# Attention followed by a mixture of experts: gating in small steps inside the next batch's attention, global scores one slot ahead, another order in the software DMA queue, six y buffers

## The chip, the cores and the metric

The kernel runs on one core of a Trainium2 chip. The metric is the time of one execution on the device in microseconds (us), the median of several runs. Two numbers appear for a run: its time, and the span of its profile from the first to the last instruction, which is about 2 us shorter. Engines are called PE (TensorE matmul), DVE (VectorE), ACT (ScalarE), POOL (GpSimd) and SP (SyncE).

For one core, a run is called slow when it is over 1.5% above the fastest of the same kernel. Ratios use fast runs only. They are computed as the mean time of one kernel's fast runs over the mean of the other's fast runs in the same rounds, with a 95% interval, so a ratio is not quite the ratio of the medians quoted beside it. The experiments ran on three chips, called A, B and C here, and the kernel before was timed again on each.

## The reference, cut to what matters

```python
def _attn_ref(q, k, v, n_global, n_local):       # q, k, v: (4, 8, 768, 64) fp32
    ...
    keep = is_global | is_local                  # 8 global keys, 96 local ones (causal)
    ...                                          # bias by distance and head, softmax
    return np.matmul(a, v)

def _moe_ref(x, w_skip, w_gate, w1, w2):         # x: 3072 rows of 512
    do_compute = x @ w_skip > 0                  # the other rows are copied
    out = x.copy()
    e_idx = np.argmax(xc @ w_gate, axis=1)       # one of 8 experts
    ...                                          # gate_w: its softmax probability
    for e in range(E):                           # w1 (8,512,1024), w2 (8,1024,512)
        h = np.maximum(xc[mask] @ w1[e], 0.0)
        y[mask] = gate_w[mask, None] * (h @ w2[e])
    out[do_compute] = xc + y
```

Rows of one batch can be gated as soon as its attention is finished. The experts need the rows of all batches, because the rows of one expert come from everywhere.

## The kernel before

There are 16 attention units, one for each batch and pair of heads (`n` counts units, `hp` the pair within the batch `b`). Each unit has transposes of q and k, three score steps and two value steps. A value step writes rows to `xb`. When a batch is complete, SP writes its rows to DRAM (`x_out`), and during the next batch's units its rows are gated: `logits` (transposes and copies, three pieces), then `gate` and `place` as one block each. `place` turns the ranks of the rows into expert slots (`slot_ps`). `skip_out` scatters 128 finished rows to the output.

```python
    for n in range(NU):                          # NU = 16
        b, hp = units[n]
        if hp == 0:
            global_scores(b)                     # both halves, as the batch begins
        m, j = n + 4, n + 2
        ...                                      # scores(j, 0)
        values(n, 0)
        ...                                      # scores(j, 1), transposes(m, 1)
        if b > 0 and hp < 3:
            logits(b - 1, hp)
        ...                                      # scores(j, 2)
        values(n, 1)
        ...                                      # transposes(m, 0), loads
        if hp == HP - 1:
            x_out(b)
        if b > 0 and hp == 2:
            gate(b - 1)
        for _ in range(2):
            if skips:
                skip_out(skips.pop(0), "first")
        if b > 0 and hp == 3:
            gate_rest(b - 1)
            place((b - 1) * T, T, colid_i, gat_pool, ps_ms, "ms")
            skips += range((b - 1) * T, b * T)
```

For each expert, 256 slots are gathered from DRAM (`gather`, two indirect DMAs), transposed on PE (`xp`, copied to `xt`), multiplied by w1 (`hps`, then `ht`) and by w2 (`yps`). DVE adds the gated result to the row in `y`, and an indirect DMA scatters `y` to the output. Weights are loaded in halves of 1 MB after conversion to bf16. Eight halves are loaded during attention and eight late. Every gather, scatter and weight load is issued by GpSimd, in program order.

```python
    def expert(e, xt, rows, gate_, group):
        ...                                      # 4 times: hps (8 matmuls), Relu to ht
        for c in range(2):
            yps = ps_y.tile([128, DM], FP32, tag="yps", name="yps")     # 3 buffers
            ...                                  # 8 matmuls
            y = ffn.tile([128, DM], FP32, tag="y", name="y", bufs=4)
            ...                                  # DVE: y = yps * gate + xg
            put(nc.gpsimd.indirect_dma_start(    # scatter y to the output
                ...), group)

    def experts(group, first):
        rows, src, gate_ = slot_rows()
        for e in range(E):
            gather(e, src)
            if first and e % 2 == 1:
                for i in range(2):
                    load_half(2 * (E - 4) + e - 1 + i, wearly if e == 1 else wlate)
        xt = expert_in(0)
        for e in range(E):
            nxt = expert_in(e + 1) if e + 1 < E else None
            expert(e, xt, rows, gate_, group)
            if first:
                if e > 0 and e < 4:
                    for t in range(NT - T + 2 * e - 2, NT - T + 2 * e):
                        skip_out(t, group)
            xt = nxt
```

The softmax here doesn't subtract the row's maximum and nothing guards it: scores larger than these inputs give would overflow.

## Time and profile before

| | before |
|---|---|
| median of the first three runs | 234.59 us (234.57 to 235.47) |
| span of the profiled run | 234.0 us |
| last `xb` written (attention ends) | starts at 113.23 us |
| last gating ends (`slot_ps` of batch 3) | 126.95 us |
| first gather issued | 129.33 us |
| first matmul of expert 0 | 137.20 us |
| last `y` | starts at 221.03 us |

The page's rows below divide the span in 40 slices of 5.85 us. A digit is the busy share of a slice in tenths; PEclk is the granted TensorE clock.

```profile
span 234.0 us, 4720 instructions
...
PEclk9999997699758985598575559999965569999975
DMA  5999999999999999999960299999999633311110
GB/s 82 145 173 187 181 139 157 236 161 146 158 196 243 211 236 230 246 237 241 274 168 20 67 155 211 241 215 229 222 201 222 183 105 123 104 64 45 40 43 0
```

The DMA row is full from the second slice to about 117 us, nearly empty from 123 to 135 us (20 and 67 GB/s, the last gating and the first gathers), and full again until about 181 us. The windows show the hole in two stretches; the columns are the start and end, the length, the busy time of the engines, the granted clock, the DMA share and GB/s.

```profile
core 0: us, PE busy (x) PEld busy (x) DVE busy (x) ACT busy (x) POOL busy (x), PEclk, DMA share, GB/s
...
122.00:127.00 5.00, 0.38 (x9) 0.30 (x10) 4.41 (x19) 0.24 (x1) 0.21 (x1) 0.63 0.14 34
127.00:132.00 5.00, 0.53 (x6) 0.34 (x6) 1.25 (x10) 0.00 (x0) 2.06 (x3) 0.50 0.09 26
```

The view of waits gives who waited for whom: total us, number of waits, longest.

```profile
ACT g_sb L279 <- PE gp L276: 19.8, 8, 6.1
PE yps L613 <- DVE y L618: 19.5, 1, 19.5
POOL out_dram L482 <- DMA w<-in_moe_w_dram: 17.9, 5, 4.2
...
PE slot_ps L472 <- DVE oha L466: 14.4, 4, 3.9
...
PE rk_ps L411 <- DVE ohb L406: 8.5, 4, 2.7
```

`gp` are the global scores, `oha` and `ohb` are the serial chain of gating. In the attention stage PE stands for them because each gating block is a run of small DVE instructions with a matmul at its end. The 19.5 us wait is one single stop of PE. The chain of waits that ended last shows where it comes from (start, duration, what ran):

```profile
151.26 17.66 DMA w<-in_moe_w_dram
168.96 0.54 issue
169.73 17.81 DMA out_dram<-y,rows
187.66 0.76 DVE y L618
188.47 3.40 PE yps L613 x8
```

The `y` of expert 0 was computed at 144.17 and 145.90 us. Its scatter was issued only at 169.73 us, because GpSimd first had to issue all gathers and all late weights, and it waited for room in the queue (about 4 us at a time). It landed at 187.5 us. The fifth `y` had to wait for that landing, and PE waited for the fifth `y`.

One more view matters later: the PE timeline where the experts begin (start, duration, instruction, idle time before it and its releaser).

```profile
132.17 0.61 PE L593 MATMUL xp<-ident,xg 128*128 128x128 bf16 x4 [4.64 <-DMA xg<-x_rows,src]
134.22 1.12 PE L593 MATMUL xp<-ident,xg 128*128 128x128 bf16 x8 [1.43 <-DMA xg<-x_rows,src]
136.80 0.61 PE L593 MATMUL xp<-ident,xg 128*128 128x128 bf16 x4 [1.47 <-DMA xg<-x_rows,src]
137.20 5.20 PE L606 MATMUL hps<-xt,w 128*128 128x256 bf16 x32
```

PE is in program order, and the program has the transposes of expert 1 ahead of the first matmul of expert 0. The rows of an expert come in two halves. The first line is the first half of expert 0's rows, the second line is its second half together with the first half of expert 1's, and the third is the second half of expert 1's. So expert 0 starts 5.0 us after the first half of its own rows has come and 3.0 us after the second half, when expert 1's are there too.

### The profile page before, as it was taken

What the parts mean: (1) busy time and instruction counts of PE and PEld (TensorE: products, weight loads), DVE (VectorE), ACT (ScalarE), POOL (GpSimd) and SP (SyncE); (2) the same over time, 40 slices, a digit from 0 to 9 for tenths busy, and PEclk for the clock granted to TensorE, in tenths of its full rate; (3) what the DMA queues carried; (4) which work ended last, traced back from release to release, by engine and by line L of the source; (5) the groups of instructions that cost most, each with busy time, mean ns of one, the idle gap of its engine ahead of it and who ended that gap; (6) DMA issues with size and microseconds to landing.
All of it is one profiled execution on the core that took longest, in us unless ns stands there. A gap on an engine that the chain in (4) does not pass through costs nothing.

```text
span 234.0 us, 4720 instructions
## 1 busy us (share of the span) xinstructions
PE 150.0 (64%) x1877; PEld 106.2 (45%) x1877; DVE 108.5 (46%) x341; ACT 91.3 (39%) x144; POOL 112.1 (48%) x139
## 2 busy tenths in 40 slices
PE   1569995985769757695451179699800079999700
PEld 1445771764527645365451155566600046776400
DVE  7554996498845888478838021130000061232300
ACT  5865982893518935293030013223400004433200
POOL 8765596666572232641360775633436057333210
PEclk9999997699758985598575559999965569999975
DMA  5999999999999999999960299999999633311110
GB/s 82 145 173 187 181 139 157 236 161 146 158 196 243 211 236 230 246 237 241 274 168 20 67 155 211 241 215 229 222 201 222 183 105 123 104 64 45 40 43 0
DMA packets 50521, 38.25 MB, mean 163 GB/s; under 512 B 30276, under 2 KB 39492, under 8 KB 50496
## 3 DMA queue, kind: packets, MB, share of 16 engines
q0 software_dynamic: 45568, 34.62, 94.4%
q1 hardware_dynamic: 4928, 3.30, 5.5%
q8 instruction: 16, 0.26, 0.5%
q14 instruction: 9, 0.07, 0.1%
HBM read 54.68 MB, written 13.63 MB: 292 GB/s over the span
## 4 chain that ended last, share of the span: by engine, by line
DMA 30%; PE 25%; DVE 20%; ACT 9%; issue 6%; POOL 5%; POOLq 0%; ACTq 0%; DVEq 0%
DMA out_dram<-y,rows 8%; DMA w<-in_moe_w_dram 8%; PE yps L613 7%; DMA kr<-in_k_dram 6%; PE hps L606 6%; DMA xg<-x_rows,src 5%; DVE xb L346 4%; DVE a L315 4%; DMA qr<-in_q_dram 4%; PE gp L276 3%; ACT xts L376 3%; ACT a L301 3%; ACT a L309 3%; POOL xg L585 2%; DVE qt L255 2%
## 5 line engine op out<-in xcount | busy, mean ns | idle before, releaser
L609 ACT ACTIVATE ht<-hps 128x512 bf16<-128x512 f32 x32 | 19.1, 597 | 76.8 <-PE hps L606 76.8
L613 PE MATMUL yps<-w,ht 128*128 128x512 bf16 x128 | 30.6, 393 | 19.5 <-DVE y L618 19.5
L618 DVE SCALAR_TENSOR_TENSOR y<-yps,gate,xg 128x512 f32<-128x512 f32 x16 | 11.9, 750 | 65.8 <-PE yps L613 34.4
L482 POOL DMA_INDIRECT out_dram<-xb,skip_k x24 | 25.0, 1042 | 35.1 <-DMA w<-in_moe_w_dram 17.9
L315 DVE TENSOR_TENSOR a<-a,mask 128x896 bf16<-128x896 bf16 (+1 forms) x48 | 28.3, 590 | 18.7 <-ACT a L301 11.2
L301 ACT ACTIVATE a<-sc 128x896 bf16<-128x896 f32 x32 | 28.9, 924 | 8.7 <-PE sc L296 7.7
L621 POOL DMA_INDIRECT out_dram<-y,rows x16 | 15.7, 981 | 33.2 <-DVE y L618 23.4
L606 PE MATMUL hps<-xt,w 128*128 128x256 bf16 x256 | 30.8, 281 | 0.0
L613 PEld LDWEIGHTS <-ht 128*128 128x128 bf16 x128 | 12.9, 100 | 34.0 <-issue 21.5
L606 PEld LDWEIGHTS <-w 128*128 128x128 bf16 x256 | 25.6, 101 | 3.7
L585 POOL DMA_INDIRECT xg<-x_rows,src x16 | 15.6, 976 | 22.0 <-DMA w<-in_moe_w_dram 11.6
L97 POOL DMA_DIRECT2D vb<-in_v_dram x24 | 21.4, 903 | 6.7 <-DVE vb L93 2.5
L296 PE MATMUL sc<-qt,kt 64*128 64x224 bf16 x192 | 19.6, 293 | 3.1 <-ACT a L301 1.3
L333 PE MATMUL av<-vb,a 128*128 128x65 bf16 x192 | 19.3, 208 | 0.0
L340 PE MATMUL av<-vb,a 128*96 128x65 bf16 x160 | 18.5, 220 | 0.0
L346 DVE TENSOR_TENSOR xb<-av,rc 128x384 bf16<-128x384 f32 x32 | 17.8, 558 | 1.1
L333 PEld LDWEIGHTS <-a 128*128 128x128 bf16 x192 | 17.2, 118 | 0.0
L340 PEld LDWEIGHTS <-a 128*96 128x96 bf16 x160 | 15.8, 139 | 0.0
L376 ACT ACTIVATE xts<-xt_ps 128x1024 bf16<-128x1024 bf16 x11 | 11.3, 1030 | 10.0 <-PE xt_ps L369 9.7
L251 PE MATMUL tr<-ident,kr 96*64 96x96 bf16 x256 | 10.9, 243 | 6.5 <-DMA kr<-in_k_dram 6.5
L88 POOL DMA_DIRECT2D qr<-in_q_dram x16 | 10.4, 649 | 8.3 <-PE sc L296 3.5
L259 ACT ACTIVATE kt<-tr 128x768 bf16<-128x768 bf16 x16 | 13.0, 814 | 1.7 <-PE tr L251 1.7
(117 smaller groups left out, 221.0 us busy)
## 6 DMA issues: line engine op xcount, KB each, us to landing
w<-in_moe_w_dram POOLq DMA_DIRECT2D x16, 1024.0 KB, 18.9
kr<-in_k_dram POOLq DMA_DIRECT2D x16, 192.0 KB, 7.9
qr<-in_q_dram POOLq DMA_DIRECT2D x16, 192.0 KB, 7.8
vb<-in_v_dram POOLq DMA_DIRECT2D x24, 128.0 KB, 8.7
x_rows<-xb SPq DMA_DIRECT2D x4, 768.0 KB, 8.9
out_dram<-xb,skip_k POOLq DMA_INDIRECT x24, 10.0
xg<-x_rows,src POOLq DMA_INDIRECT x16, 12.3
out_dram<-y,rows POOLq DMA_INDIRECT x16, 2.7
```

Of the source, the lines that this page charges most:

```text
L97: nc.gpsimd.dma_start(out=vbs[b][:, t, :, 0:D], in_=v_r[b, t])
L296: nc.tensor.matmul(out=sc[:, hh, kk, 0:R * wp].rearrange("a (r p) -> a r p", r=R), lhsT=kt[rows, t * 128:(t + 1) * 128], rhs=qt[rows, :, t ...
L301: nc.scalar.activation(out=a[:, :, :].rearrange("a h (k p r) -> a h k p r", k=2, r=R), in_=sc[:, :, :, 0:W].rearrange("a h k (r p) -> a h ...
L315: nc.vector.tensor_tensor(out=a[:, :, 0:wid], in0=a[:, :, 0:wid], in1=m[:, :, 0:wid], op=ALU.mult)
L333: nc.tensor.matmul(out=av[:, jj, hh, :], lhsT=a_sbs[n, t // 2][:, hh, (t % 2) * W:(t % 2) * W + 128], rhs=vb[:, t, h, :], start=False, sto ...
L340: nc.tensor.matmul(out=av[0:NL, jj, hh, :], lhsT=a_sbs[n, p // 2][:, hh, c:c + NL], rhs=vb[:, p, h, :], start=False, stop=(jj == 2 and hh ...
L346: nc.vector.tensor_tensor(out=xb[:, 3 * u:3 * u + 3, 2 * hp * D:(2 * hp + 2) * D].rearrange("p j (h d) -> p j h d", h=2), in0=av[:, :, :, ...
L482: put(nc.gpsimd.indirect_dma_start(out=out[:, :], out_offset=bass.IndirectOffsetOnAxis(ap=skip_k[:, t:t + 1], axis=0), in_=xbs[t // T][:, ...
L585: nc.gpsimd.indirect_dma_start(out=xg[e][:, c, :], out_offset=None, in_=x_dram[:, :], in_offset=bass.IndirectOffsetOnAxis(ap=src[:, 2 * e ...
L606: nc.tensor.matmul(out=hps[:, j, :], lhsT=w1_sb[e][:, dc, c2 * 256 + j:(c2 + 1) * 256:2], rhs=xt[:, dc, :], start=(dc == 0), stop=(dc == D ...
L609: nc.scalar.activation(out=ht[:, c2, :, :], in_=hps[:, :, :], func=ACT.Relu)
L613: nc.tensor.matmul(out=yps[:, :], lhsT=ht[:, f // 2, f % 2, c * 128:(c + 1) * 128], rhs=w2_sb[e][:, f // 2, (f % 2) * DM:(f % 2 + 1) * DM] ...
```

## The change

The intent has four parts. Gating becomes a generator of small steps, and each attention unit takes three of them, between its own steps, so that the serial chain fills holes instead of making them. The global scores of the next batch are computed in the last unit of the batch before, which needs transposes five units ahead (`LEAD`) instead of four. In the expert part, only six experts' gathers and the weights of experts 4 to 6 are issued at once; those of experts 6 and 7 and the last weights come after the `y` of expert 0. And `y` has six buffers.

```diff
-    def global_scores(b):
+    def global_scores(b, u):                     # one half per call
...
+    def gating(b):                               # logits, gate, place, gate_rest
+        for s in range(3):
...
+            yield
...                                              # further steps, each ends with a `yield`
-    for n in range(4):
+    LEAD = 5
+    for n in range(LEAD):
...
     for n in range(NU):
         b, hp = units[n]
-        if hp == 0:
-            global_scores(b)
-        m, j = n + 4, n + 2
+        m, j = n + LEAD, n + 2
...
+        if hp == 3 and b + 1 < B:
+            global_scores(b + 1, 0)
+        next(side, None)
         values(n, 0)
...
-        if b > 0 and hp < 3:
-            logits(b - 1, hp)
+        if hp == 3 and b + 1 < B:
+            global_scores(b + 1, 1)
+        next(side, None)
...
         values(n, 1)
+        next(side, None)
...
-        if b > 0 and hp == 2:
-            gate(b - 1)
...
-        if b > 0 and hp == 3:
-            gate_rest(b - 1)
-            place((b - 1) * T, T, colid_i, gat_pool, ps_ms, "ms")
+        if hp == HP - 1:
+            x_out(b)
+            for _ in side:                       # what is left of the batch before
+                pass
+            side = gating(b)
...
-            y = ffn.tile([128, DM], FP32, tag="y", name="y", bufs=4)
+            y = ffn.tile([128, DM], FP32, tag="y", name="y", bufs=6)
...
-        for e in range(E):
-            gather(e, src)
-            ...                                  # two late halves after each odd e
+        fetch(0, 8)                              # gathers of experts 0 and 1, halves 8, 9
+        fetch(2, 10)
+        fetch(4, 12)
         xt = expert_in(0)
         for e in range(E):
             nxt = expert_in(e + 1) if e + 1 < E else None
             expert(e, xt, rows, gate_, group)
-            if first:
-                if e > 0 and e < 4:              # 2 skip scatters each
+            if e == 0:
+                fetch(6, 14)
+            if first and e >= 3:                 # 2 skip scatters each
```

## The prediction

> What bounds it now. Three stretches, from the timeline, the waits and the 40 slices (span 234.0 us).
>
> (a) Attention, to 116.9 us. A unit of batch 0 takes about 3.55 us with VectorE full. Batches 1 and 2, which also carry gating, take 29 us each (gp matmuls at 38.9, 67.0, 96 us), although VectorE is busy for only about 20.5 (windows). The holes: PE waits for ohb (8.5 us over four gatings) and for oha (14.4), ACT waits for gp (19.8 over eight). Behind this stands a second limit: the DMA row reads 9 tenths from 6 us to 117, and GpSimd waits for room in the one software queue (17.9 us "out_dram <- DMA w").
>
> (b) Last gating, 116.9 to 127.5 us, then the first gather at 129.3 and the first expert at 137.2: DMA nearly idle (20 and 67 GB/s).
>
> (c) Experts: 7.4 us each on a warm PE, but PE stands 19.5 us (from 168.9): the fifth y needs one of four buffers; expert 0's rows were computed at 144.2 but their scatter was issued at 169.7, behind all gathers and late weights, and landed at 187.5. Last scatter issued at 222.1, 12 us before the end.
>
> The change only moves work. Gating steps fill VectorE and PE holes: I estimate batches 1 and 2 at 22 to 23 us each, from the 20.5 us of VectorE; the last xb at about 98 to 101 instead of 113.8. One more unit in the prologue delays the first values by 2 to 3 us. The last gating is unchanged (10.6 us), so slots are ready near 110 instead of 127.5. But the queue still has the same bytes to move before the gathers; in before it is drained only at about 121. By the Trainium skill ("DMA: Bandwidth & Descriptors", Anatomy of one DMA) DMA engines do not wait on semaphores but consume their queues; the trace agrees (weights issued at 151.3 landed 17.7 us later). So I expect the gathers issued near 111 but landed near 122 to 125, and expert 0 near 125 instead of 137: 12 us gained, 8 more hidden behind DMA.
>
> Experts, as an estimate from the trace (half a weight 4.8 us of queue, a gather 0.75, a y scatter 1.2): queue order now is six gathered experts and w of 4 to 6, then y of expert 0, then expert 7. Its y lands near 162, y of expert 1 near 177. With six y and three yps buffers PE runs without a stop into expert 5, stands there 5 to 9 us instead of 19.5, and ends near 194 to 196 instead of 221. So 12 to 14 us gained here.
>
> Prediction: 209 us (11% faster), range 200 to 219. Faster by over 2% 0.97, within 2% 0.02, slower 0.01.
>
> Right if: the waits show yps<-y under 10 us and the wait for the y scatter after expert 2, not 1; PE's oha and ohb waits fall from 23 us to under 8 outside the last gating; the DMA row has no hole near 120 to 130; the first xp transposes come at 120 to 127. Wrong if: the two ms PSUM buffers, with rk held over two steps, stall the transposes so that batches stay at 27 us or more; q and k, needed a unit sooner, arrive late (DMA waits at the tr transposes); the queue drains well before 120, which gives up to 8 us more; or y scatters land later than estimated, so the stall stays near 19 us.

## The result, and the profile after

| | before | after |
|---|---|---|
| median of four runs in the same rounds | 234.58 us (233.47 to 235.47) | 217.32 us (214.63 to 218.0) |
| ratio of fast runs | | 0.9197 (0.9095 to 0.9299) |
| span of the profiled run | 234.0 us | 212.8 us |
| last `xb` starts | 113.23 us | 107.38 us |
| `slot_ps` of batch 3 | 126.95 us | 117.81 us |
| first gather issued | 129.33 us | 122.08 us |
| first matmul of expert 0 | 137.20 us | 130.15 us |
| last `y` starts | 221.03 us | 200.11 us |

Two of the four runs after the change, 218.0 and 217.89 us, count as slow against the fastest; the profiled run, 214.63 us, is that fastest one. The profiled run before, 235.85 us, is not among those of the median and lies 1.3 us above it. So the profile shows 21.2 us of gain where the medians show 17.3. Of the 21.2 us in the spans, 7.05 come before the first expert matmul (137.20 to 130.15), 13.9 in the expert stage (83.8 to 70.0 us from the first `hps` to the last `y`), and 0.3 in the tail.

The rows of the page after; a slice is now 5.32 us long:

```profile
span 212.8 us, 4715 instructions
...
PEclk9999889699799995895567555899999997599955
DMA  4999999999999999999999749999999999333100
GB/s 70 143 179 176 203 152 111 165 165 232 166 152 189 225 236 243 231 230 262 220 244 277 177 103 162 212 240 212 236 208 256 199 199 301 120 113 96 49 34 0
```

The hole between attention and experts has become a dip (7 and 4 tenths, 177 and 103 GB/s). It has not closed:

```profile
122.00:127.00 5.00, 0.74 (x6) 0.48 (x7) 0.00 (x0) 0.00 (x0) 4.00 (x5) 0.50 0.42 108
127.00:132.00 5.00, 3.27 (x21) 2.31 (x20) 1.38 (x2) 0.00 (x0) 4.09 (x5) 0.50 0.83 134
```

The waits that answer to those of before:

```profile
POOL out_dram L493 <- DMA w<-in_moe_w_dram: 27.1, 8, 4.8
...
PE rk_ps L447 <- DVE ohb L441: 6.9, 4, 2.3
...
PE slot_ps L391 <- DVE oha L382: 6.6, 4, 3.7
ACT g_sb L280 <- PE gp L277: 6.4, 6, 1.8
...
PE yps L622 <- DVE y L627: 5.8, 1, 5.8
```

Every wait that the change aimed at has shrunk, and one that it did not aim at has grown: at its skip scatters GpSimd waits longer for room in the queue (17.9 to 27.1 us). Part of that has only moved there from the gathers, whose wait of this kind fell from 11.6 to 3.8 us; over all its instructions it grew from 32.8 to 40.3 us. The reason was not tested. The chain of waits around the start of the experts and around the stop of PE:

```profile
101.69 18.65 DMA out_dram<-xb,skip_k
120.45 0.35 issue
120.80 0.71 POOL out_dram L493
121.51 0.57 issue
122.08 1.01 POOL xg L594
...
174.68 1.74 PE yps L622 x8
176.42 5.00 issue
181.42 0.76 DVE y L627
182.23 3.51 PE yps L622 x8
```

The scatter of expert 1's first rows, and the `y` of expert 4 that needs its buffer, from the timelines of GpSimd and DVE:

```profile
168.29 1.04 POOL L630 DMA_INDIRECT out_dram<-y,rows  x1 [0.45 <-issue]
181.42 1.41 DVE L627 SCALAR_TENSOR_TENSOR y<-yps,gate,xg 128x512 f32<-128x512 f32 x2 [11.82 <-issue]
```

The first gather now comes behind batch 2's skip scatters, the last of which GpSimd could issue only at 120.8 us. The rest of PE's stop is in expert 5 instead of expert 3. There the `y` of expert 4 waits for the landing of expert 1's rows. The views name no releaser for this wait ("issue"), but with six buffers the ninth `y` needs the buffer of the third, and that one's scatter landed 13.1 us after its issue, at 181.3 us. Expert 0's scatters were issued at 149.76 and 154.79 us and landed by 167.7 us.

The attention stage by batch, from the start of the last `xb` of each batch in the DVE timeline:

| batch | before ends at | took | after ends at | took |
|---|---|---|---|---|
| 0 | 37.80 | 37.80 | 43.66 | 43.66 |
| 1 | 63.08 | 25.28 | 67.02 | 23.36 |
| 2 | 92.13 | 29.05 | 90.27 | 23.25 |
| 3 | 113.23 | 21.10 | 107.38 | 17.11 |

Batches 1 to 3 gain 11.7 us together, and batch 0, which now also holds one more unit of transposes and the global scores of batch 1, gives back 5.9. That is 5.9 us in all. Slots were ready 9.1 us earlier, and the other 3.3 us come from the gating of batch 2: in before its `slot_ps` ran at 116.28 us, after the last `xb`, and held up the gating of batch 3; after the change it ran at 107.29 us, just before the last `xb`. The gating of batch 3 itself, from its first transposes to its `slot_ps`, took 10.3 us before and 10.1 us after. The PE timeline where the experts begin:

```profile
124.91 0.61 PE L602 MATMUL xp<-ident,xg 128*128 128x128 bf16 x4 [6.52 <-DMA xg<-x_rows,src]
126.87 1.16 PE L602 MATMUL xp<-ident,xg 128*128 128x128 bf16 x8 [1.35 <-DMA xg<-x_rows,src]
129.75 0.61 PE L602 MATMUL xp<-ident,xg 128*128 128x128 bf16 x4 [1.73 <-DMA xg<-x_rows,src]
130.15 5.71 PE L615 MATMUL hps<-xt,w 128*128 128x256 bf16 x32
```

### The profile page after: what moved, and what is told of

Its sections match the earlier page's. It is cut to its first block, busy times and chain, and to the rows that moved or that the text cites. A ratio compares the mean times of both kernels' runs of the same rounds, so it can differ in the third digit from the quotient of the medians.

```text
span 212.8 us, 4715 instructions
## 1 busy us (share of the span) xinstructions
PE 149.1 (70%) x1877; PEld 106.4 (50%) x1877; DVE 107.5 (51%) x341; ACT 90.9 (43%) x144; POOL 112.1 (53%) x139
## 4 chain that ended last, share of the span: by engine, by line
DMA 34%; PE 29%; issue 11%; POOL 10%; DVE 7%; ACT 4%; POOLq 0%; DVEq 0%; ACTq 0%
PE yps L622 12%; PE hps L615 11%; DMA w<-in_moe_w_dram 9%; DMA out_dram<-xb,skip_k 9%; DMA vb<-in_v_dram 7%; DMA xg<-x_rows,src 5%; DMA qr<-in_q_dram 4%; POOL out_dram L493 3%; POOL xg L594 2%; DVE a L318 2%; ACT a L304 1%; DVE xb L349 1%; PE xp L602 1%; PE tr L251 1%; DVE qt L255 1%
## 5 line engine op out<-in xcount | busy, mean ns | idle before, releaser
L493 POOL DMA_INDIRECT out_dram<-xb,skip_k x24 | 24.8, 1035 | 39.6 <-DMA w<-in_moe_w_dram 27.1
L304 ACT ACTIVATE a<-sc 128x896 bf16<-128x896 f32 x32 | 29.3, 923 | 14.8 <-PE sc L299 14.2
L318 DVE TENSOR_TENSOR a<-a,mask 128x896 bf16<-128x896 bf16 (+1 forms) x48 | 28.1, 586 | 13.6 <-ACT a L304 7.2
L615 PE MATMUL hps<-xt,w 128*128 128x256 bf16 x256 | 31.3, 284 | 0.0
L336 PE MATMUL av<-vb,a 128*128 128x65 bf16 x192 | 20.1, 211 | 0.0
L343 PE MATMUL av<-vb,a 128*96 128x65 bf16 x160 | 19.4, 226 | 0.0
L336 PEld LDWEIGHTS <-a 128*128 128x128 bf16 x192 | 17.8, 121 | 0.0
L343 PEld LDWEIGHTS <-a 128*96 128x96 bf16 x160 | 16.7, 144 | 0.0
L251 PE MATMUL tr<-ident,kr 96*64 96x96 bf16 x256 | 11.1, 245 | 6.5 <-DMA kr<-in_k_dram 6.1
L328 PE MATMUL av<-vg,g_sb 128*128 128x130 bf16 x96 | 12.6, 249 | 2.1 <-DVE vg L218 1.2
L602 PE MATMUL xp<-ident,xg 128*128 128x128 bf16 x64 | 6.2, 242 | 11.1 <-DMA xg<-x_rows,src 11.1
## 6 DMA issues: line engine op xcount, KB each, us to landing
w<-in_moe_w_dram POOLq DMA_DIRECT2D x16, 1024.0 KB, 18.5
out_dram<-xb,skip_k POOLq DMA_INDIRECT x24, 11.7
```

The source lines that it names most:

```text
L304: nc.scalar.activation(out=a[:, :, :].rearrange("a h (k p r) -> a h k p r", k=2, r=R), in_=sc[:, :, :, 0:W].rearrange("a h k (r p) -> a h ...
L318: nc.vector.tensor_tensor(out=a[:, :, 0:wid], in0=a[:, :, 0:wid], in1=m[:, :, 0:wid], op=ALU.mult)
L336: nc.tensor.matmul(out=av[:, jj, hh, :], lhsT=a_sbs[n, t // 2][:, hh, (t % 2) * W:(t % 2) * W + 128], rhs=vb[:, t, h, :], start=False, sto ...
L343: nc.tensor.matmul(out=av[0:NL, jj, hh, :], lhsT=a_sbs[n, p // 2][:, hh, c:c + NL], rhs=vb[:, p, h, :], start=False, stop=(jj == 2 and hh ...
L493: put(nc.gpsimd.indirect_dma_start(out=out[:, :], out_offset=bass.IndirectOffsetOnAxis(ap=skip_k[:, t:t + 1], axis=0), in_=xbs[t // T][:, ...
L615: nc.tensor.matmul(out=hps[:, j, :], lhsT=w1_sb[e][:, dc, c2 * 256 + j:(c2 + 1) * 256:2], rhs=xt[:, dc, :], start=(dc == 0), stop=(dc == D ...
```

## The experiments

All kernels gave the reference's result. The theory was that the change is two independent gains: attention ends earlier, and the expert stage is shorter because expert 0's rows land earlier and because six buffers reach further. The rival was that the two overlap, so that either alone gives most of the gain, or that only one of queue order and buffers works.

### Chip A: the halves of the change, and the parts of the expert half

The first four ran together; the kernel before took 236.22 us there (235.05 to 237.49, seven runs).

**Expert part alone** (before, with the new `experts` and six `y` buffers):

```diff
     gate_rest(B - 1)
+    skips = list(range(NT - T, NT))
     attn.close()
...
-    y = ffn.tile([128, DM], FP32, tag="y", name="y", bufs=4)
+    y = ffn.tile([128, DM], FP32, tag="y", name="y", bufs=6)
...                                              # experts(): the lines of the change
```

> The kernel before with only the change's expert part (last two experts' gathers and weights queued after expert 0's rows, six y buffers, skip scatters from expert 3 on). Theory (two independent gains, the PE stall is one of them): expert 0 starts at 137 us as before, PE's wait yps<-y falls from 19.5 us to 4 to 8, time 220 to 222. Rival (all gain comes from the earlier end of attention; the queue holds the same bytes, so the stall only moves): wait stays over 15 us, time 231 to 235.

Measured: 222.14 us (220.81 to 222.86), ratio 0.9397 (0.9333 to 0.9462). The first `hps` started at 136.61 us, as in before, and the stop of PE was 6.1 us. The theory holds; the time is 0.1 us above its 220 to 222 us.

**Attention part alone** (after, with the old `experts` and four `y` buffers; the edit is that of the run above, reversed, on the other kernel):

```diff
-    y = ffn.tile([128, DM], FP32, tag="y", name="y", bufs=6)
+    y = ffn.tile([128, DM], FP32, tag="y", name="y", bufs=4)
...                                              # experts(): the lines of before
```

> The changed attention and gating with the expert part of before (all gathers and late weights first, four y buffers). Theory: the first matmul of expert 0 at 130 us instead of 137, the stall yps<-y stays 18 to 21 us, time 226 to 229. Rival (the queue's bytes alone set when expert 0's rows land): the y scatter lands at 187 as before, the stall grows to about 26 us, time 233 to 235.

Measured: 230.57 us (229.31 to 234.65, that last run slow), ratio 0.9744 (0.9664 to 0.9823). The first `hps` came at 131.32 us and the stop of PE was 19.7 us, as in before (19.5 us). The time is above the theory's 226 to 229 us, on a chip where the kernel before is 1.6 us slower than in the first pair. The product of the two ratios, 0.9397 x 0.9744 = 0.916, is near the 0.9197 of the whole change. The gains are independent: the earlier end of attention moves the expert stage as a whole, and does not change what happens in it.

**Four y buffers** (after, one line):

```diff
-            y = ffn.tile([128, DM], FP32, tag="y", name="y", bufs=6)
+            y = ffn.tile([128, DM], FP32, tag="y", name="y", bufs=4)
```

> The changed kernel with four y buffers instead of six. Theory (order and buffers are both needed): the rows of expert 1 land at about 181, PE then stands a whole expert earlier, stall 11 to 15 us in all, time 223 to 226. Rival (the order in the queue does it alone): stall near 6 us, time 216 to 219.

Measured: 222.69 us (221.35 to 224.15), ratio 0.9414 (0.9336 to 0.9491). PE stopped twice, 5.45 us for expert 0's rows and 3.15 us for expert 1's. That is 8.6 us, less than the 11 to 15 that the theory expected, so the size was missed on this run.

```profile
169.22 3.57 PE L622 MATMUL yps<-w,ht 128*128 128x512 bf16 x8 [5.45 <-DVE y L627]
182.72 3.57 PE L622 MATMUL yps<-w,ht 128*128 128x512 bf16 x8 [3.15 <-DVE y L627]
```

**Old queue order** (after with six buffers, but with all gathers and weights ahead of the first `y`):

```diff
         fetch(4, 12)
+        fetch(6, 14)
         xt = expert_in(0)
...
-            if e == 0:
-                fetch(6, 14)
```

> The changed kernel with six y buffers, but the gathers and weights of experts 6 and 7 queued before expert 0's rows, as before. Theory: rows of expert 0 land near 180, PE stands from about 170 in expert 4 for 10 to 13 us, time 222 to 226. Rival (the buffers do it alone): stall near 6 us, time 216 to 219.

Measured: 223.98 us (223.23 to 225.39), ratio 0.9498 (0.9432 to 0.9563). The PE timeline has one stop, before the last half of expert 4's results:

```profile
182.95 3.57 PE L622 MATMUL yps<-w,ht 128*128 128x512 bf16 x8 [11.88 <-DVE y L627]
```

Expert 0's rows landed at 182.15 us. The theory holds. With the other traces this gives a small table. The landing is read at the start of the first `y` that waited for it and counted from the issue of the first gather, the length from the first `hps` to the last `y`:

| kernel | queue order | y buffers | expert 0's rows landed after | PE stops for y | expert stage |
|---|---|---|---|---|---|
| before | old | 4 | 58.3 us | 19.5 us | 83.8 us |
| attention alone | old | 4 | 58.4 us | 19.7 us | 84.2 us |
| order alone ("four y buffers") | new | 4 | 44.0 us | 8.6 us | 76.9 us |
| buffers alone ("old queue order") | old | 6 | 57.7 us | 11.9 us | 76.6 us |
| experts alone | new | 6 | 45.5 us | 6.1 us | 70.6 us |
| after | new | 6 | 45.5 us | 5.8 us | 70.0 us |

The landing depends on the queue order alone, not on the number of buffers or on the time at which the stage begins. Two more buffers let PE work one expert longer before it stops: 7.6 us (84.2 to 76.6), near the 7.4 us of one warm expert. The order gives 7.3 us, and both together 13.6 to 14.2 us, so on these single traces they nearly add (14.9). The order brings the landing 14.4 us forward (58.4 to 44.0) but the stage only 7.3 us, for two reasons. With four buffers PE then stops 3.15 us more for the next landing, expert 1's, 57.5 us after the first gather, so the stops shrink by 11.1 us. The other 3.8 us go to slower matmuls: the granted clock was 0.50 for the first 3.5 us after each of the two stops, and 0.77 and 0.76 over the `hps` that follow. From the restart to the next expert's first `yps` PE took 8.45 and 8.53 us, where a warm PE takes about 5.7 (an estimate: one expert of 7.4 us less half of its `yps`). That is 5.7 us lost, against 1.8 after the one stop of "attention alone" (7.48 us). So a stop cost more than its length here, and that the gains nearly add is an observation and not a rule. One thing the table doesn't separate: the two kernels with the order or the buffers alone also have the skip scatters of the new kernel, from expert 3 on.

### Chip B: can the experts start earlier?

The kernel before took 244.01 us here (242.63 to 244.84, seven runs), so only ratios compare with chip A.

**The change again, as a control:**

> The changed kernel itself, as the control for the runs beside it. Both theories: ratio to before 0.91 to 0.93, gathers issued at 122 to 125 us, stall yps<-y 5 to 7 us in expert 5.

Measured: 223.07 us (221.06 to 224.26), ratio 0.9153 (0.91 to 0.9205). The ratio of the change holds on a chip where everything is slower, and the gathers were issued at 124.53 us, as expected. The stall did not come as expected: PE's wait for `y` was 1.3 us and not 5 to 7. The `y` of expert 4 was again released about 13 us after the scatter of expert 1's first rows was issued (170.47 and 183.62 us), but PE was already late, because it had waited for `ht` of ACT; and the expert stage took 74.1 us instead of 70.0. The trace also shows irregular waits whose releaser is unknown: DVE 3.8 us once and ACT 4.8 us in three waits. They are taken up at the end.

**Batch 2's skip scatters moved behind the gathers**, because in the trace after the change they stand just before the first gather:

```diff
-    while skips:
-        skip_out(skips.pop(0), "first")
     for _ in side:
         pass
...
-            if first and e >= 3:
-                for _ in range(2):
+            if first and e >= 2:
+                for _ in range(3):
```

> The changed kernel with the six skip scatters of batch 2 moved from before the gathers into the expert stage. Theory (the gathers are held up on GpSimd behind skip scatters that wait for room in the queue): gathers issued at 119 to 121, as soon as the slots are known, expert 0 starts 2 to 5 us earlier, the end follows, time 2 to 5 us under the control. Rival (the gathers are bound by the last gating alone, and the moved scatters delay the y rows): start within 1 us, time equal or up to 4 us over the control.

Measured: 228.74 us (224.09 to 232.97), ratio 0.9369 (0.9274 to 0.9464), which is 2.4% above the control's. The first gather was issued 2.4 us after `slot_ps` of batch 3 (121.06 and 123.44 us). In the control that distance is also 2.4 us (122.12 and 124.53 us). So on this chip the skip scatters did not hold the gathers up at all: there was nothing to gain, and the run can't test what they cost where they do. In the first profile the distance is 4.27 us (117.81 and 122.08 us), so they held the gathers up for 1.9 us there, and on chip A by 1.3 and 3.1 us in the runs with four buffers and with the old order (3.67 and 5.46 us). Here the gathers are bound by the last gating, and the scatters moved into the expert stage go with a longer stage (78.1 us against 74.1). Two of the four runs are slow, so the size is uncertain. The rival holds on this chip.

**The next expert's transposes between the halves of an expert**, so that expert 0 needs only its own rows:

```diff
-    def expert(e, xt, rows, gate_, group):
+    def expert(e, xt, rows, gate_, group, mid):
...                                              # after the Relu loop:
+        nxt = mid()
         for c in range(2):
...
-            nxt = expert_in(e + 1) if e + 1 < E else None
-            expert(e, xt, rows, gate_, group)
+            nxt = expert(e, xt, rows, gate_, group,
+                         lambda: expert_in(e + 1) if e + 1 < E else None)
```

> The changed kernel with the transposes of the next expert's rows placed between the two halves of an expert instead of before it, so that expert 0 doesn't wait for the gathers of expert 1. Theory (the stage ends when rows of expert 1 have landed, plus two and a half experts; a head start is given back there): expert 0 starts near 128 instead of 130, expert 1 near 138 instead of 141, the stall grows from 6 to 8 to 10 us, time within 1.5 us of the control. Rival (PE's own chain from expert 0 sets the end): time 2 to 4 us under the control.

Measured: 221.47 us (218.72 to 223.07; three fast runs), ratio 0.9009 (0.8927 to 0.9091) against 0.9153 of the control. Counted from the first gather, expert 0 started after 6.6 instead of 7.9 us and expert 1 after 16.7 instead of 19.4 us; the last `y` came after 80.7 instead of 82.0 us. The order of PE's program does cost time at the start. In the trace PE's stops for `y` grew from 1.3 to 6.1 us, so part of the head start was given back, as the theory says; but the time is below the control's, as the rival says. The intervals of the two ratios nearly touch (0.9091 and 0.91), and the last `y` gained 1.3 us where the ratios differ by 3.5 us. The size stays open between the two.

**Seven y buffers** (a kernel with eight does not build, for want of SBUF):

```diff
-            y = ffn.tile([128, DM], FP32, tag="y", name="y", bufs=6)
+            y = ffn.tile([128, DM], FP32, tag="y", name="y", bufs=7)
```

> The changed kernel with seven y buffers instead of six (eight don't fit in SBUF). Theory (PE stands in expert 5 only for want of a y buffer until the rows of expert 1 land at about 181): one more half expert may run, the stall yps<-y falls from 5.8 us to under 3, time 3 to 6 us under the control. Rival (the queue is the limit of the whole stage, late weights or scatters stop PE elsewhere): another wait of about the same size, time within 1.5 us of the control.

Measured: 221.98 us (217.48 to 226.9), with three of four runs slow. There is no ratio and the run is inconclusive.

### Chip C: the parts of the attention half, and the best version

The kernel before took 242.66 us here (242.2 to 244.09, seven runs). The first two kernels have the whole expert part of the change.

**Small steps alone** (four units ahead, global scores at the start of their own batch):

```diff
-    LEAD = 5
+    LEAD = 4
...
-        if n == 3:
-            for u in range(2):
-                global_scores(0, u)
...
+        if hp == 0:
+            for u in range(2):
+                global_scores(b, u)
...                                              # the two calls at hp == 3 are removed
```

> The changed kernel with gating in small steps, but with four units transposed ahead as before and the global scores at the batch's first unit, as before. Theory (the small steps carry most of what attention gained): last slot placement 1 to 4 us later than in the changed kernel (117.8), first values near 22 instead of 24.8, ratio to before 0.92 to 0.94. Rival (the global scores one slot ahead carry it): placement after 122, ratio over 0.945.

Measured: 224.36 us (223.11 to 225.11), ratio 0.9213 (0.9165 to 0.9262). The ratio is inside the theory's range. ACT waited 15.2 us for the global scores again, and the last `slot_ps` came at 124.16 us, later than the expected 119 to 122; but that range was set on the first pair, and the control on chip B has it at 122.12 us. Batch 0 ended at 38.22 us, as in before (37.80), so the 5.9 us that it gives back after the change do come from the fifth unit and the early scores together; their shares are not shown.

```profile
ACT g_sb L280 <- PE gp L277: 15.2, 8, 4.9
```

**Scores ahead alone** (gating in blocks as before):

```diff
             global_scores(b + 1, 0)
-        next(side, None)
         values(n, 0)
...
-        next(side, None)
+        if hp < 3:
+            next(side, None)
...
         values(n, 1)
-        next(side, None)
...
+        if hp == 2:
+            for _ in range(5):
+                next(side, None)
```

> The changed kernel with the global scores one slot ahead and five units transposed ahead, but gating in blocks, at the same places as before. Theory (small steps carry the gain): last slot placement at 123 to 127 us, PE waits for ohb and oha stay over 18 us in sum, ratio to before 0.94 to 0.97. Rival: placement before 121, ratio under 0.935.

Measured: 230.86 us (230.07 to 232.03), ratio 0.9505 (0.9451 to 0.956). The last `slot_ps` came at 131.13 us (expected was 123 to 127), and PE waited 14.1 us for `oha` and 10.4 us for `ohb`, near the 14.4 and 8.5 us of before.

```profile
PE slot_ps L391 <- DVE oha L382: 14.1, 4, 3.9
PE rk_ps L447 <- DVE ohb L441: 10.4, 4, 3.5
```

Between these two runs, on one chip, `slot_ps` differs by 7.0 us and the medians by 6.5. So of the two parts the small steps carry the gain of the attention half. The scores ahead, added to them, bring about 0.6 per cent (0.9213 to 0.9153, and that across chips), which is inside the scatter. The kernel with neither part (experts alone, 0.9397) and that with both ran on other chips only. Their wait shrank (19.8 to 6.4 us in the first pair of profiles), but batch 0 pays for it.

**Seven y buffers again:**

> The seven y buffers alone once more, since the chip of the first run showed waits of ACT for an unknown releaser in every kernel. Theory: stall yps<-y under 3 us, ratio to before 0.89 to 0.905. Rival: another wait of the same size takes its place, ratio 0.91 to 0.925.

Measured: 219.65 us (217.87 to 221.24; three fast runs), ratio 0.9012 (0.8935 to 0.9089). The ratio is in the theory's range. The wait of PE for `y` is gone from the waits. The profiled run was a slow one, so its times are not used beyond that; and since the control on chip B waited only 1.3 us for `y`, the missing wait alone does not say how much the seventh buffer is worth.

**Seven y buffers and expert 0 first** (the edits of both):

```diff
+        nxt = mid()
...
-            y = ffn.tile([128, DM], FP32, tag="y", name="y", bufs=6)
+            y = ffn.tile([128, DM], FP32, tag="y", name="y", bufs=7)
```

> Seven y buffers and the next expert's transposes between the two halves of an expert, both on the changed kernel; the version meant to beat both. Theory (a head start for expert 0 counts only when the y buffers no longer stop PE): expert 0 near 128, stall yps<-y under 4 us, ratio to before 0.87 to 0.90. Rival (queue bytes set the end anyway): ratio 0.905 to 0.925, as the changed kernel.

Measured: 218.34 us (217.05 to 218.82), ratio 0.8965 (0.8917 to 0.9013). The theory's ratio and stall came true; expert 0 started at 132.1 us and not near 128. This is the fastest version measured: 10.4% below before, and about 2% below the change, if the ratios of chips B and C are compared (0.9153 and 0.8965). The change itself did not run on chip C, so the 2% is a comparison across chips. On chip C itself it is 0.5% ahead of seven buffers alone (0.8965 and 0.9012), with intervals that overlap: what the order of the transposes adds to the seventh buffer is not shown. PE no longer waits for `y`. The wait has moved. Two lines of the DVE timeline and one of PE's show it:

```profile
184.84 0.75 DVE L628 SCALAR_TENSOR_TENSOR y<-yps,gate,xg 128x512 f32<-128x512 f32 x1 [11.80 <-issue]
185.51 0.68 DVE L606 COPY xt<-xp 128x512 int32<-128x512 int32 x1
...
186.25 6.43 PE L615 MATMUL hps<-xt,w 128*128 128x256 bf16 x32 [6.25 <-DVE xt L606]
```

The second `y` of expert 4 waits on DVE. The trace names no releaser and has no landings; by the count of buffers it needs the one of expert 1's first rows, whose scatter was issued 13.1 us before, the time that this landing took in the profile after. The copy of expert 6's transposed rows stands behind it. The Trainium skill ("TensorE: Matmul & The Clock Gate", Architectural detail) calls the queue of VectorE strictly first in, first out. The trace agrees: a 0.68 us copy, which needs neither the buffer nor the landing, starts only when the `y` ahead of it is released, and PE pays 6.25 us for it.

## Why the prediction was right or wrong

The measured 217.32 us is inside the predicted range of 200 to 219 us, near its upper end. The gain was predicted as 25.6 us and is 17.3 us in the medians. Point by point:

**The expert stage was right, in mechanism and in size.** "So 12 to 14 us gained here": the stage became 13.9 us shorter. The remaining stop, predicted as 5 to 9 us in expert 5, is 5.82 us in expert 5. "Ends near 194 to 196" was 70 us after the predicted start of expert 0 at 125, and the stage took 70.0 us. The landings, predicted near 162 and 177 us, came at 167.6 and 181.4 us. Counted from the start of expert 0 that is 37 and 52 us predicted against 37.5 and 51.3 measured. The runs with one part each show that both causes named, order and buffers, are needed (PE stopped 8.6 and 11.9 us with one of them, 5.8 us with both).

**The step that failed is "expert 0 near 125 instead of 137: 12 us gained".** It compares two different events. The gathers were expected to land near 122 to 125 us, and the first did: it landed at 124.86 us and the first `xp` ran at 124.91 us. But the 137 us of before is the first matmul of expert 0, and before's first `xp` was at 132.17 us. The 5.0 us between them, in which the second half of expert 0's rows and then expert 1's land and are transposed, were in the trace of before and are 5.2 us after. So the gain at this point was 7.05 us and not 12. The run with expert 0 first shows that the order in PE's program is a part of these 5 us: with it reversed, expert 0 started 1.3 us and expert 1 2.7 us earlier after the first gather.

That the landing came out right was luck. The gathers were to be issued near 111 us and to stand 11 to 14 us in a full queue. They were issued at 122.08 us, because slots were ready later than forecast, and the first landed 2.8 us later, as in before (129.33 and 132.13 us). Once they were issued, the queue did not hold them.

The forecast also reckoned with "a warm PE". The Trainium skill ("TensorE: Matmul & The Clock Gate", What's actually happening) states a half-rate clock after an idle window. This agrees, with 0.50 granted from 127 to 132 us in both kernels, and 0.69 and 0.63 on average during the 32 `hps` matmuls of expert 0, which took 5.2 and 5.7 us against 3.66 us for those of expert 1. The prediction left this cost at the start of the expert stage out; it is nearly the same before and after.

**The step before it failed too, and its own terms did not give its sum.** "The last xb at about 98 to 101 instead of 113.8": it started at 107.4 us. The two batches took 23.4 and 23.3 us, close to the predicted 22 to 23. The cost of the longer prologue was predicted as 2 to 3 us: the first values came 3.1 us later (21.68 to 24.82 us), but by the end of batch 0 it was 5.9 us; the global scores of batch 1, which moved into that batch, are the likely rest, but their share was not measured. And the terms as written never gave 98 to 101. From before's two intervals of 57.1 us (38.9 to 96 us, `gp` to `gp`), two batches of 22 to 23 us save 11 to 13, less 2 to 3 is 8 to 11, so 103 to 106 us.

**"8 more hidden behind DMA" was mis-sized.** Slots were ready 9.1 us earlier, not the 17.5 that the text assumed. Behind the queue, 1.9 us were hidden: the gathers came 4.27 us after `slot_ps` in the profile of after, where 2.4 us is the distance in before. In the other runs of the changed attention it was 0 to 3.1 us. As a check, the failed terms explain the miss of 8.3 us: 12 us predicted at the start of the experts against 7.05 is 5 us, of which the expert stage and the tail give 0.6 back, and the remaining 4.0 us lie between the profiled runs and the medians (2.7 us after, 1.3 us before).

**Of the signs that were to show it right,** the stop under 10 us, the wait after expert 2 and the first `xp` at 120 to 127 us came true. PE's waits for `oha` and `ohb` fell less than asked: 22.9 us became 13.5 us, of which the last gating alone has about 5 us (one wait of 3.7 for `oha`, about 1.5 for `ohb`), which leaves about 8.3 outside it. That sign, "under 8", was missed narrowly. "The DMA row has no hole near 120 to 130" did not come true: it dips to 7 and 4 tenths there, with 108 GB/s from 122 to 127 us against 34 in before. None of the named dangers appeared. The two `ms` PSUM buffers did not hold the batches at 27 us.

On the Trainium skill's statement used in the prediction ("DMA: Bandwidth & Descriptors", Anatomy of one DMA) that DMA engines consume their queues and do not wait on semaphores: the runs fit it, but none tests it by itself. The landing of expert 0's rows went with the order of issue in the queue and not with the other parts that were changed (57.7 to 58.4 us in the old order, 44.0 to 45.5 in the new). The fit of the same section, about 2.0 us plus the bytes over 436 thousand per us, gives as an estimate 4.4 us for the 1 MB that a half of a weight has in bf16, and 6.8 us for the 2 MB that it has in fp32 before. The measured median from issue to landing was 18.9 us in before and 18.5 in after. The fit is given per DMA; here the rest, most of the time, went by behind what stood ahead in the queue, by the order of issue and landing above.

Another section matters for reading such a page: the skill ("Perfetto Trace Analysis", DMA Instruction — SWDGE) says that the profile's end of such an instruction is the end of descriptor generation and not of the movement. The trace agrees: each scatter of `y` occupies GpSimd for about 1.0 us (0.97 to 1.05), while its landing comes 2.3 to 17.7 us after the issue. Whoever reads only the busy time of the POOL group sees 16 us of work and misses the wait.

## What to carry to other kernels

When an engine stops for a buffer that a DMA must empty, what counts is the landing of that write, and it is set by the write's place in the queue: put short writes that free buffers ahead of bulk loads that are not needed soon, and count buffers up to the landing (the one pair added here was worth 7.6 us, about one expert). A serial chain of small instructions is best cut into steps between other work; here that was nearly all of the attention gain, as far as runs on different chips can say, and hoisting work into an earlier batch brought little. When a gain is predicted from a trace, subtract the same event on both sides, for a landing is not yet a start, and add the written terms once more.

## What the Trainium skill lacked or had wrong

- "DMA: Bandwidth & Descriptors", Anatomy of one DMA, gives the cost of one DMA by itself (4.4 us by its fit for 1 MB, an estimate) but not how to reckon with a queue that is full. Here the median from issue to landing was 18.5 to 18.9 us for that size, and GpSimd stood still for up to 4.8 us at a time, 27.1 us in total in the skip scatters alone, where the view of waits names a weight load ahead as the releaser.
- The same page says nothing on the order of reads and writes in the software queue as a tool of scheduling. Moving two experts' gathers and 2 MB of weights behind two scatters brought the landing of these from 58 to 44 or 45 us after the first gather.
- No page that was used explains the waits on DVE and ACT for an unknown releaser. They appeared in the traces of chips B and C (DVE 3.8 us and ACT 4.8 us in the control; 8.9 us for one copy in the best version) and not in the first pair or on chip A. Nor does one explain why the kernel before took 234.6, 236.2, 244.0 and 242.7 us in the four series of runs (the first pair of kernels, chips A, B and C). Both stay open.
